# Two chained feed-forward layers after pooled attention: converted words in their own place, sums on VectorE, loads in another order

## The chip, the core and the metric

The kernel runs on one core of a Trainium2 chip. The metric is the device time of one execution in microseconds (us), as the median of three timed runs. A separate execution was taken with the hardware profiler, and all rows below are from that one.

## What is computed

Attention with keys and values that are first averaged over groups of eight positions, then two feed-forward layers, each a product, an activation and a second product:

```python
x = attention(q, mean8(k), mean8(v))          # 4608 tokens x 512
h = x @ w_in;   g = np.maximum(0.01 * h, h);  x = g @ w_out      # d_ff 2048
h = x @ w_in2;  g = np.where(h >= 1, h, np.where(h <= -1, 0.0, (h + 1) ** 2 / 4))
out = g @ w_out2
```

The weights come in as 64-bit words and are converted on the chip. Each value is split into a high part that TensorE can take and the rest, so one product is three matmuls: high by high, low by high, high by low.

## The kernel before

The program is one list of instructions written out by hand, in four phases. The first (to 574.5 us) does attention and x @ w_in block by block. The second (`Blocks.run` of layer 0) does g @ w_out, the third (`Second.first_phase`) x @ w_in2, the fourth (`Blocks.run` of layer 1) g @ w_out2. The last three use a scheme with 7 products of half blocks in place of 8; it needs sums and differences of quarter blocks beside the products.

**Second and fourth phase.** The 4608 tokens are four pairs of 512-column blocks (r = 0 to 3) and one pair of 256-column blocks, called the short pair here (r = 4). A pair has 7 positions (one product each, order `ORDER2`) of 8 units, so 56 units; a unit is 6 matmuls of 512 columns in the second phase, 12 of 256 in the fourth, and 6 of 256 in either short pair. In step u of `run` the program issues unit u's matmuls, then `hi(u + 5)` (ScalarE rounds the source, L1084), then `lo(u + 4)` (VectorE subtracts, L1089), then a sum of quarter blocks for a later unit (`g_sum`): for even f, and for all f of the first pair, VectorE adds in place 7 units ahead (L1069); for odd f of the other pairs GpSimd issues a DMA that accumulates, 10 units ahead (L1067). `g_load` (L1050) brings activations from DRAM, `fetch` (L1009) weights. After each product, `post` copies or adds its banks into output tiles (`out_tile`, places `spare[0]` to `spare[3]`) and stores them.

**Conversion beside the second phase.** `during(u)` converts w_out2 in 32 halves, one every 5 units: `bits_load` (L98) into a tile of the pool `raw`; 3 units later `convert`, whose first two steps are ScalarE's (L630, L631), then three of VectorE (L633 to L637) and one of GpSimd (L641); then `f32_store` (L146). `convert` writes into a second tile of the same pool, which has three buffers, so a later load waits until an earlier half's store has landed. In the short pair `during` also prepares the third phase: weights (`w1_fetch`, L723), `x_load`, sums (`x_sum`, GpSimd, L761) and splits (`x_split`, L718, L719).

**Third phase.** Six pairs of 768 columns with 8 cycles each, 48 cycles; a cycle has 7 slots, one product of 6 matmuls of 384 columns each. `after(cycle, slot)` holds the copies, additions (L885) and activations (L899, L904, L910) of a slot and the stores of their results (L913); `put(cycle, slot, ...)` adds work to a slot behind these. Put there are: the remaining weights `w1_fetch(12)` to `(27)`; `x_load`, `x_sum` and `x_split` for the next pair; and the sums and splits of w_out2, two of its eight parts f per pair: `w2_load` (L774), 5 slots later `w2_sums` (four on GpSimd, L783 to L786), from 7 slots on seven times `w2_split` (ScalarE L615, VectorE L618 or L620, store L797), one per slot; two tiles hold two splits each, so the fifth waits for the store of the first two. The end of the phase loads the fourth's first weights and activations.

Engines take their instructions in the program's order, SyncE (SP) its DMAs too: a DMA whose source or place is not ready holds all later ones.

Of the kernel before, what the change touches and what calls it, by code (L numbers as in the profile page):

```python
# [17 lines left out]
P = 128  # L18
# [15 lines left out]
STORES_LATE = 6  # L34

# [4 lines left out]
def attention_moe_moe2(ctx: ExitStack, tc: tile.TileContext, qT, kT, v, k01, v01, w_in1, w_out1, w_in2, w_out2, out):  # L40
# [648 lines left out]
    class Second:  # L689
# [6 lines left out]
        def __init__(self, free):  # L696
# [9 lines left out]
            self.n_t = self.n_x2 = 0  # L706
# [105 lines left out]
        def during(self, u):  # L812
            i, step = divmod(u - 7 * self.NJ + 4, 5)
            job = self.halves[i] if 0 <= i < len(self.halves) else None
            if step == 0:
                if 0 < i <= len(self.halves):
                    next(self.turn)
                if job:
                    bits_load(*job, raw_tile)
            elif step == 1 and 0 < i <= len(self.halves):  # L820
                f32_store(*self.halves[i - 1])
            elif step == 3 and job:
                self.turn = convert(*job, raw_tile)
                next(self.turn)
            elif step == 4 and job:
                next(self.turn)
# [5 lines left out]
            for at, f, *args in (  # L832
# [9 lines left out]
                if n == at:  # L842
                    f(*args)

# [70 lines left out]
        def first_phase(self):  # L915
            for t in range(EARLY, 28):
                self.put((t - EARLY) // 4 - 1, 1 + (t - EARLY) % 4, self.w1_fetch, t)
            for p in range(1, self.NPAIR):
                c = self.NJ * (p - 1)
                for cycle, slot, f, *args in (  # L920
                    (4, 2, self.x_load, p),
                    (5, 2, self.x_split, p, 0, 0), (5, 3, self.x_split, p, 0, 1),
                    (5, 4, self.x_sum, 1), (5, 6, self.x_sum, 3), (6, 1, self.x_sum, 2),
                    (6, 2, self.x_split, p, 2, 0), (6, 3, self.x_split, p, 2, 1), (6, 4, self.x_sum, 4),
                    (6, 4, self.x_split, p, 1, 0), (6, 6, self.x_split, p, 1, 1),
                    (7, 0, self.x_split, p, 3, 0), (7, 1, self.x_split, p, 3, 1),
# [499 lines left out]
```

## Time and profile before

| | |
|---|---|
| timed runs | 1677.17, 1678.49, 1684.18 us, median 1678.49 |
| profiled execution | 1684.41 us, of it span 1682.6 us |
| busy TensorE (PE), VectorE (DVE), ScalarE (ACT), GpSimd (POOL) | 1621.6, 1189.0, 975.9, 476.1 us |
| matmuls | 9324 |
| mean granted TensorE clock | 0.989 |

The busy time of PE counts a matmul from its start to its modelled end, also where it was slow; so the time that can be won is read from how many matmuls a stretch holds and the pace at which undisturbed ones follow each other. The chain of waits is the work that ended last, followed back from the end. A row of the timeline merges neighbours of one line (xN), with the time from the first's start to the last's end.

### The profile page before, as it was taken

To read this page: it belongs to the slowest core of one execution; us is meant where nothing else is said; L and a number is where in the kernel's file an instruction comes from. 1 tells how busy PE (TensorE), PEld (TensorE's weight loads), DVE (VectorE), ACT (ScalarE), POOL (GpSimd) and SP (SyncE) were. 2 spreads that over 40 slices of the span, in tenths; PEclk is the share of its full clock that TensorE was granted. 3 is DMA by queue.
4 is the path that set the end of the run, shared out by engine and by line. 5 is a ranking of instruction groups with operands and counts; after the bars stand their busy time and mean duration, and the time that the engine had idled before them with its cause. 6 is when DMAs were issued, how large, how long until landed. Compare 5 with 4: busy or idle time off the path is not lost.

```text
span 1682.6 us, 28605 instructions
## 1 busy us (share of the span) xinstructions
PE 1621.6 (96%) x9324; PEld 1449.2 (86%) x9324; DVE 1189.0 (71%) x2351; ACT 975.9 (58%) x2113; POOL 476.1 (28%) x604
## 2 busy tenths in 40 slices
PE   6899999999999999999998999999999899999998
PEld 4678787788788888888787899999999899999998
DVE  6968877877863388989786556765664786766766
ACT  4656555556554345665554577887776545454545
POOL 3524433443431004443334221221110012232323
PEclk9999999999999999999999999999999999999999
DMA  7557776778666798897869676556347977777744
GB/s 220 179 162 245 240 240 226 253 234 254 224 210 222 297 338 226 243 254 235 232 181 291 254 258 221 184 201 234 126 152 238 344 261 177 202 157 207 154 126 104
DMA packets 229973, 370.48 MB, mean 220 GB/s; under 512 B 26752, under 2 KB 108672, under 8 KB 229824
## 3 DMA queue, kind: packets, MB, share of 16 engines
q1 hardware_dynamic: 211392, 339.30, 60.2%
q0 software_dynamic: 18432, 29.37, 10.7%
q8 instruction: 73, 1.20, 0.3%
q14 instruction: 76, 0.62, 0.1%
HBM read 196.61 MB, written 142.61 MB: 202 GB/s over the span
## 4 chain that ended last, share of the span: by engine, by line
PE 71%; DVE 11%; DMA 9%; issue 3%; ACT 3%; POOL 2%; SPq 1%; DVEq 0%; ACTq 0%; POOLq 0%
PE u L1126 21%; PE u L1117 14%; PE Y L866 6%; PE h L587 6%; PE h L588 6%; PE h L589 6%; PE V L866 4%; PE X L866 4%; DMA m<-g 2%; DMA w2x<-wdo 1%; PE sc L431 1%; DMA w2d<-w2o 1%; DMA wb1o<-in_moe_w_out_dram 1%; PE tm L490 1%; DVE m L1089 1%
## 5 line engine op out<-in xcount | busy, mean ns | idle before, releaser
L1089 DVE TENSOR_TENSOR m<-m,m 128x512 fp32r<-128x512 f32 (+1 forms) x560 | 383.5, 699 | 176.4 <-ACT m L1084 163.6
L1084 ACT ACTIVATE m<-m 128x512 fp32r<-128x512 f32 (+1 forms) x560 | 324.9, 588 | 314.3 <-PE u L1126 147.5
L1126 PE MATMUL u<-v,m 128*128 128x256 f32 x3024 | 365.4, 284 | 3.5 <-ACT m L1084 3.3
L1126 PEld LDWEIGHTS u<-v,m 128*128 128x128 f32 x3024 | 364.6, 193 | 4.3 <-ACT m L1084 3.5
L1117 PE MATMUL u<-m,v 128*128 128x512 f32 (+1 forms) x1680 | 353.6, 372 | 9.8 <-ACT m L1084 5.6
L1117 PEld LDWEIGHTS u<-m,v 128*128 128x128 f32 x1680 | 296.2, 190 | 67.2 <-DVE m L1089 7.8
L587 PE MATMUL h<-xh,w0i 128*128 128x512 f32 x448 | 183.1, 409 | 0.8 <-ACT t L595 0.8
L588 PE MATMUL h<-xl,w0i 128*128 128x512 f32 x448 | 176.4, 394 | 1.8 <-DVE xl L175 1.8
L589 PE MATMUL h<-xh,w0i 128*128 128x512 f32 x448 | 176.3, 394 | 0.0
L1067 POOL DMA_DIRECT2D m<-m x128 | 112.3, 1101 | 174.0 <-DVE m L1089 148.2
L595 ACT ACTIVATE t<-h 128x512 f32<-128x512 f32 x144 | 86.0, 597 | 121.2 <-PE h L589 63.6
L1234 POOL TENSOR_TENSOR o<-o,o 128x512 f32<-128x512 f32 x36 | 62.2, 1754 | 323.9 <-DVE o L1228 323.8
L1069 DVE TENSOR_TENSOR m<-m,m 128x512 f32<-128x512 f32 (+1 forms) x192 | 127.5, 664 | 0.0
L467 POOL TENSOR_TENSOR at<-at,r 128x32 f32<-128x32 f32 (+3 forms) x160 | 72.1, 472 | 156.1 <-DVE r L464 124.4
L587 PEld LDWEIGHTS h<-xh,w0i 128*128 128x128 f32 x448 | 85.0, 190 | 20.2 <-issue 1.8
L589 PEld LDWEIGHTS h<-xh,w0i 128*128 128x128 f32 x448 | 84.7, 189 | 18.6
L588 PEld LDWEIGHTS h<-xl,w0i 128*128 128x128 f32 x448 | 84.9, 189 | 17.8 <-DVE xl L175 2.7
L866 PE MATMUL Y<-xs,v 128*128 128x384 f32 x432 | 87.2, 339 | 5.9 <-DVE p L885 4.6
L866 PE MATMUL X<-xs,v 128*128 128x384 f32 x432 | 86.7, 335 | 0.6 <-ACT Y L879 0.6
L866 PE MATMUL V<-xs,v 128*128 128x384 f32 x432 | 86.6, 334 | 0.0
L866 PEld LDWEIGHTS Y<-xs,v 128*128 128x128 f32 x432 | 75.9, 189 | 8.8 <-DVE p L885 6.2
L885 DVE TENSOR_TENSOR q<-V,q 128x384 f32<-128x384 f32 x48 | 26.6, 555 | 80.3 <-ACT q L879 80.3
(261 smaller groups left out, 2732.5 us busy)
## 6 DMA issues: line engine op xcount, KB each, us to landing
m<-g SPq DMA_DIRECT2D x256, 256.0 KB
g<-t SPq DMA_DIRECT2D x144, 256.0 KB
m<-m POOLq DMA_DIRECT2D x96, 256.0 KB, 5.5
wf<-v0o SPq DMA_DIRECT2D x56, 256.0 KB
wi<-v1i SPq DMA_DIRECT2D x56, 256.0 KB
v<-wf SPq DMA_DIRECT2D x28, 512.0 KB
v<-wi SPq DMA_DIRECT2D x28, 512.0 KB
w2d<-w2o SPq DMA_DIRECT2D x56, 256.0 KB
```

The lines of the kernel that those rows point to most:

```text
L467: nc.gpsimd.tensor_tensor(out=t, in0=t, in1=r[0:n].to_broadcast([n, 4, w]), op=ALU.mult)
L587: nc.tensor.matmul(ph, wh[:, c], xh, start=k == 0, stop=False)
L588: nc.tensor.matmul(ph, wh[:, c], xl, start=False, stop=False)
L589: nc.tensor.matmul(ph, wl[:, c], xh, start=False, stop=k == KT - 1)
L595: nc.scalar.activation(out=t, in_=h_t.pop(f), func=AF.Prelu, alpha=0.01)
L866: nc.tensor.matmul(ps, w[:, c], x[k, i], start=begin and k == n == 0, stop=k == 1 and n == 2, skip_group_check=True,)
L1067: nc.gpsimd.dma_start(out=t, in_=x, accum_op=ALU.add)
L1069: nc.vector.tensor_tensor(out=t, in0=x, in1=t, op=ALU.add)
L1084: nc.scalar.activation(out=self.s[u][0], in_=self.unit_source(u), func=AF.Copy)
L1089: nc.vector.tensor_tensor(out=lo, in0=self.unit_source(u), in1=hi, op=ALU.subtract)
L1117: nc.tensor.matmul(banks[b][:, at:at + n], w[:, c], x, start=fresh and at == 0 and i == 0, stop=end and i == 2, skip_group_check=True,)
L1126: nc.tensor.matmul(ps, a[:, c], w, start=fresh and tt % 2 == 0 and i == 0, stop=end and i == 2, skip_group_check=True,)
```

## The change

Five edits, all in phases two to four; TensorE's instructions and their order stay as they are. (1) `convert` in `during` writes into a tile of its own, `cuts` (two halves, in `spare[3]`), and the load of a half is issued 8 units ahead of `convert` rather than 3; the output tile that stood in `spare[3]` goes to `spare[0]` (`i % 3`). (2) In the short pair all sums are VectorE's, in both layers. (3) `w1_fetch(12)` to `(27)` come one every 2.5 slots instead of four a cycle; the w_out2 work moves from pairs 0 to 3 to pairs 1 to 4, with one slot more between load, sums and splits; `x_load`, sums and splits move up to 3 slots. (4) The fourth phase's first weights come one every 5 slots, its first `g_load`s one per slot, and 11 of them (`FIRST`) two per unit in the first six units. (5) In layer 1 the weights of `run` come at f = 4 to 7 rather than 0 to 3.

```diff
+FIRST = [((2, 1), f) for f in (5, 6, 7)] + [((1, 1), f) for f in range(8)]
@@ during
-            i, step = divmod(u - 7 * self.NJ + 4, 5)
...
+            for at, what in ((0, "load"), (8, "convert"), (9, "next"), (10, "next"), (11, "store")):
+                i, step = divmod(u - 7 * self.NJ + 8 - at, 5)
...
+                    bits_load(*job, raw_tile)
+                elif what == "convert":
+                    self.turn = convert(*job, self.cut_tile)
...
+        def cut_tile(self, shape, dt, name):
+            if self.cuts is None:
+                self.cuts = wpool.tile([P, 2, 512], dt, tag=self.spare[3], name="cuts")
+            self.n_cut += 1
+            return self.cuts[:, self.n_cut % 2]
@@ first_phase
-                self.put((t - EARLY) // 4 - 1, 1 + (t - EARLY) % 4, self.w1_fetch, t)
+                n = 5 * (t - EARLY) // 2
+                self.put(n // 7 - 1, n % 7, self.w1_fetch, t)
...
-                    (6, 2, self.x_split, p, 2, 0), (6, 3, self.x_split, p, 2, 1), (6, 4, self.x_sum, 4),
+                    (6, 2, self.x_split, p, 2, 0), (6, 3, self.x_split, p, 2, 1),
+                    (6, 5, self.x_split, p, 1, 0), (6, 6, self.x_split, p, 1, 1), (7, 0, self.x_sum, 4),
...
-                n = 7 * self.NJ * (f // 2) + 13 * (f % 2) + 3
-                for at, step, *args in ((0, self.w2_load), (5, self.w2_sums), *((7 + i, self.w2_split, i) for i in range(7))):
+                n = 7 * self.NJ * (f // 2 + 1) + 14 * (f % 2) + 3
+                for at, step, *args in ((0, self.w2_load), (6, self.w2_sums), *((8 + i, self.w2_split, i) for i in range(7))):
...
+            for t in range(8):
+                n = 6 + 5 * t
+                self.put(self.STEPS - self.NJ + n // 7, n % 7, self.b2.fetch, t)
             for f in range(self.NJ):
-                self.put(*((end - 3, f) if f < 4 else (end - 1, 2)), self.b2.g_load, 0, (2, 2), f)
-                self.put(end - 1, 3 if f < 4 else 6, self.b2.g_load, 0, (2, 1), f)
+                self.put(*((end - 3, f) if f < 4 else (end - 1, (2, 3, 5, 6)[f - 4])), self.b2.g_load, 0, (2, 2), f)
+            for f in range(5):
+                self.put(end, (1, 2, 4, 5, 6)[f], self.b2.g_load, 0, (2, 1), f)
...
-            by_dma = bool(f % 2 and r)
+            by_dma = bool(f % 2) and 0 < r < self.NPAIR - 1
...
+                late = 4 * self.layer
+                if r == 0 and pos < 5 and 0 <= f - late < 4:
+                    self.fetch(4 * (pos + 2) + f - late)
+                if self.layer and 2 * u < len(FIRST):
+                    for job in FIRST[2 * u:2 * u + 2]:
+                        self.g_load(0, *job)
...
-                t = self.kept[key, r] = self.out_tile(r, i)
+                t = self.kept[key, r] = self.out_tile(r, i if self.short(r) else i % 3)
```

GpSimd's list in the second phase's short pair before (m are activations, xr and x2s the third phase's x, o outputs; a DMA here is an accumulating sum):

```order
L1067 DMA m_10_6448<-m_4_6436 128x256
L1067 DMA m_11_6450<-m_5_6438 128x256
L761 TENSOR_TENSOR xr_00_9228<-xr_00_9228 128x384
L761 TENSOR_TENSOR xr_9227<-xr_9227 128x384
L761 TENSOR_TENSOR xr_00_9228<-xr_01_9230,xr_00_9228 128x384
L761 TENSOR_TENSOR xr_9227<-xr_9227 128x384
L761 TENSOR_TENSOR x2s_9384<-xr_01_9230,xr_00_9228 128x384
L761 TENSOR_TENSOR x2s_9386<-xr_9227 128x384
L1067 DMA m_8_6444<-m_34_6452 128x256
L1067 DMA m_9_6446<-m_35_6454 128x256
L1067 DMA m_10_6448<-m_36_9020 128x256
L1067 DMA m_11_6450<-m_37_9041 128x256
```

And now:

```order
L642 TENSOR_TENSOR cuts<-cuts,wb1o_1_8802 128x256
L763 TENSOR_TENSOR xr_00_9196<-xr_00_9196 128x384
L763 TENSOR_TENSOR xr_9195<-xr_9195 128x384
L763 TENSOR_TENSOR xr_00_9196<-xr_01_9198,xr_00_9196 128x384
L763 TENSOR_TENSOR xr_9195<-xr_9195 128x384
L763 TENSOR_TENSOR x2s_9353<-xr_01_9198,xr_00_9196 128x384
L763 TENSOR_TENSOR x2s_9355<-xr_9195 128x384
L1247 TENSOR_TENSOR o_0_9114<-o_0_9114,o_2_9473 128x512 x2
```

The sixteen sums of the short pair are gone from this list (six of them stand above), and VectorE's has sixteen additions more; the same holds for the fourth phase's short pair. (Lines of the changed kernel have numbers up to 13 higher.)

SyncE's list at the start of the third phase before, behind the second phase's last store (v are weights, g the results that are stored, w2x, wdo and w2d the w_out2 work):

```order
L723 DMA v_12_9662<-wi_125 128x1024
L723 DMA v_13_9673<-wi_126 128x1024
L723 DMA v_14_9675<-wi_127 128x1024
L723 DMA v_15_9683<-wi_128 128x1024
L723 DMA v_16_9712<-wi_129 128x1024
L913 DMA g_0_6100<-tX_9691 128x384
L723 DMA v_17_9725<-wi_130 128x1024
L723 DMA v_18_9737<-wi_131 128x1024
L774 DMA w2x_9739<-wdo_7097 128x512
L775 DMA w2x_9739<-wdo_8058 128x512
L723 DMA v_19_9751<-wi_132 128x1024
L913 DMA g_8_6108<-tV_9733 128x384
```

And now:

```order
L725 DMA v_12_9622<-wi_125 128x1024
L725 DMA v_13_9642<-wi_126 128x1024
L725 DMA v_14_9658<-wi_127 128x1024
L725 DMA v_15_9669<-wi_128 128x1024
L921 DMA g_0_6100<-tX_9656 128x384
L725 DMA v_16_9702<-wi_129 128x1024
L725 DMA v_17_9721<-wi_130 128x1024
L921 DMA g_8_6108<-tV_9698 128x384
L921 DMA g_8_6108<-tW_9710 128x384
L725 DMA v_18_9754<-wi_131 128x1024
L921 DMA g_1_6101<-tX_9719 128x384
L921 DMA g_0_6100<-tY_9749 128x384
```

Between two weights there are now mostly results to store, and w2x comes eight cycles later.

SyncE's list at the end of the third phase before, behind the last tX but one (m are the fourth phase's activations, g with t results that are stored):

```order
L1050 DMA m_4_13646<-g_12_6112 128x512
L1050 DMA m_5_13648<-g_13_6113 128x512
L1050 DMA m_6_13650<-g_14_6114 128x512
L1050 DMA m_7_13652<-g_15_6115 128x512
L913 DMA g_5_6105<-tY_13629 128x384
L1050 DMA m_8_13666<-g_0_6100 128x512
L1050 DMA m_9_13668<-g_1_6101 128x512
L1050 DMA m_10_13670<-g_2_6102 128x512
L1050 DMA m_11_13672<-g_3_6103 128x512
L1050 DMA m_21_13697<-g_4_6104 128x512
L1050 DMA m_21_13697<-g_5_6105 128x512
L1050 DMA m_21_13697<-g_6_6106 128x512
```

And now:

```order
L1059 DMA m_7_13656<-g_15_6115 128x512
L921 DMA g_14_6114<-tV_13623 128x384
L921 DMA g_14_6114<-tW_13637 128x384
L1059 DMA m_8_13674<-g_0_6100 128x512
L921 DMA g_7_6107<-tX_13646 128x384
L1059 DMA m_9_13679<-g_1_6101 128x512
L921 DMA g_6_6106<-tY_13669 128x384
L1059 DMA m_10_13698<-g_2_6102 128x512
L1059 DMA m_11_13703<-g_3_6103 128x512
L1059 DMA m_21_13715<-g_4_6104 128x512
L921 DMA g_15_6115<-tV_13687 128x384
L921 DMA g_15_6115<-tW_13695 128x384
```

Before, twelve loads stand together with one store among them; now the stores of tV, tW, tX and tY stand between them.

VectorE's list in the second phase, now, from the second half converted to the third, with what each waits for (DMAHW and DMASW are landings of DMAs issued by SyncE and GpSimd):

```order
L638 SCALAR_TENSOR_TENSOR cuts_7069<-wb1o0_1_7038,cuts_7069 128x256 [waits DMAHW4_49,DVE_49]
L1098 TENSOR_TENSOR m0_24_6404<-m0_9_6446,m0_21_6392 128x512 [waits DMASW1_49,Activation_49]
L1078 TENSOR_TENSOR m0_34_6452<-m0_18_6282,m0_34_6452 128x512 [waits DMAHW5_49]
L1098 TENSOR_TENSOR m0_24_6404<-m0_10_6448,m0_24_6404 128x512 [waits Activation_49]
L1098 TENSOR_TENSOR m0_29_6457<-m0_11_6450,m0_28_6456 128x512 [waits DMASW2_49,Activation_49]
L1078 TENSOR_TENSOR m0_12_6226<-m0_18_6282,m0_12_6226 128x512 [waits DMAHW7_49]
L1098 TENSOR_TENSOR m0_31_6461<-m0_34_6452,m0_30_6460 128x512 [waits Activation_49]
L1098 TENSOR_TENSOR m0_33_6472<-m0_35_6454,m0_32_6471 128x512 [waits DMASW3_49,Activation_49]
L1078 TENSOR_TENSOR m0_12_6226<-m0_1_6320,m0_12_6226 128x512
L634 TENSOR_SCALAR cuts_7069<-cuts_7069 128x256 [waits Activation_49]
L635 TENSOR_SCALAR cuts_7069<-cuts_7069 128x256 [waits DVE_49]
L638 SCALAR_TENSOR_TENSOR cuts_7069<-wb1o1_0_7096,cuts_7069 128x256 [waits DMAHW0_49,DMAHW7_49,DVE_49,Pool_49]
```

The last step of the second half into cuts waits for one landing, that of its load; the third half's, which takes the first's place again, for two.

## Rows read from the trace of the kernel before

**Rows 1.** Busy time by stretch; the header line names the columns.

```profile
core 0: us, PE busy (x) PEld busy (x) DVE busy (x) ACT busy (x) POOL busy (x), PEclk, DMA share, GB/s
574.50:883.90 309.40, 307.44 (x1345) 253.28 (x1345) 267.90 (x436) 175.03 (x323) 99.91 (x98) 0.99 0.84 248
883.90:937.70 53.80, 45.93 (x337) 42.76 (x337) 39.17 (x85) 26.22 (x69) 24.32 (x22) 0.97 0.83 240
937.70:1009.50 71.80, 65.97 (x362) 64.75 (x362) 35.06 (x70) 48.83 (x114) 13.25 (x14) 0.95 0.79 288
1009.50:1071.10 61.60, 59.38 (x338) 58.06 (x338) 40.90 (x78) 49.40 (x118) 13.73 (x14) 1.00 0.59 205
1071.10:1131.30 60.20, 59.06 (x337) 58.02 (x336) 39.82 (x78) 49.36 (x118) 14.17 (x14) 1.00 0.61 210
1131.30:1193.90 62.60, 59.84 (x338) 57.94 (x337) 39.67 (x78) 49.21 (x118) 13.41 (x14) 1.00 0.58 202
1193.90:1252.30 58.40, 58.40 (x338) 58.26 (x337) 33.47 (x64) 45.10 (x104) 7.14 (x6) 1.00 0.40 136
1252.30:1309.20 56.90, 54.93 (x313) 53.83 (x313) 26.68 (x54) 39.88 (x91) 0.00 (x0) 1.00 0.67 224
1309.20:1320.00 10.80, 7.30 (x48) 6.53 (x47) 4.31 (x8) 5.49 (x11) 0.00 (x0) 0.91 0.81 260
...
1637.70:1678.30 40.60, 40.55 (x338) 40.34 (x337) 30.12 (x71) 22.77 (x56) 15.68 (x17) 1.00 0.53 108
```

**Rows 2.** Longest pieces of the chain of waits: start, us, what, matmuls in it.

```profile
574.71 204.01 PE u L1117 x900
...
1215.03 2.08 PE Y L866 x12
...
1318.24 360.02 PE u L1126 x2986
```

**Rows 3.** The chain of waits in the second phase, 798 to 815 us.

```profile
798.58 7.10 DMA wdo<-wc1o
805.74 8.33 DMA wb1o<-in_moe_w_out_dram
814.15 0.44 ACT wc1o L630
```

**Rows 4.** ScalarE's longest wait in 883.9 to 937.7: us, times, longest.

```profile
ACT m L1084 <- DMA m<-m: 11.6, 5, 5.0
```

**Rows 5.** VectorE's timeline in the short pair: start, us, what, idle before.

```profile
910.13 6.51 DVE L1089 TENSOR_TENSOR m<-m,m 128x256 fp32r<-128x256 f32 x7
...
929.75 1.09 DVE L1089 TENSOR_TENSOR m<-m,m 128x256 fp32r<-128x256 f32 x3
```

**Rows 6.** GpSimd's timeline in the short pair.

```profile
911.38 1.19 POOL L761 TENSOR_TENSOR xr<-xr,xr 128x384 f32<-128x384 f32 x1
...
915.98 3.57 POOL L1067 DMA_DIRECT2D m<-m  x4
```

**Rows 7.** The chain of waits at the third phase's start: start, us, what.

```profile
958.34 5.34 DMA w2d<-w2o
```

**Rows 8.** TensorE's longest wait in 937.6 to 1309.1: us, times, longest.

```profile
PE Y L866 <- DVE p L885: 7.9, 10, 1.7
```

**Rows 9.** The chain of waits in the third phase's second pair.

```profile
1026.32 4.00 DMA w2d<-w2o
...
1031.73 3.14 DMA w2x<-wdo
...
1037.79 0.70 POOL w2s L786
```

**Rows 10.** The chain of waits where the fourth phase begins.

```profile
1303.60 5.64 DMA m<-g
...
1309.30 6.51 DMA g<-tV
```

More of the change, by code (lines that the diff above doesn't have):

```diff
@@ L705, in __init__ @@
             self.w2d = [dram.tile([P, self.NJ, 2, 256], F32, name=f"w2d{pos}") for pos in range(7)]
-            self.n_t = self.n_x2 = 0
+            self.n_t = self.n_x2 = self.n_cut = 0
+            self.cuts = None
             self.plan = {}
@@ L812, in during @@
         def during(self, u):
-            i, step = divmod(u - 7 * self.NJ + 4, 5)
-            job = self.halves[i] if 0 <= i < len(self.halves) else None
-            if step == 0:
-                if 0 < i <= len(self.halves):
-                    next(self.turn)
[L818 to L826, printed above, removed]
+            for at, what in ((0, "load"), (8, "convert"), (9, "next"), (10, "next"), (11, "store")):
+                i, step = divmod(u - 7 * self.NJ + 8 - at, 5)
+                if step or not 0 <= i < len(self.halves):
+                    continue
+                job = self.halves[i]
+                if what == "load":
+                    bits_load(*job, raw_tile)
+                elif what == "convert":
+                    self.turn = convert(*job, self.cut_tile)
+                    next(self.turn)
+                elif what == "next":
+                    next(self.turn)
+                else:
+                    f32_store(*job)
             n = u - 56 * (NT // 1024)
@@ L920, in first_phase @@
                 for cycle, slot, f, *args in (
[L921 to L926 removed]
+                    (4, 4, self.x_load, p),
+                    (5, 4, self.x_split, p, 0, 0), (5, 5, self.x_split, p, 0, 1),
+                    (5, 6, self.x_sum, 1), (6, 1, self.x_sum, 3), (6, 3, self.x_sum, 2),
+                    (6, 2, self.x_split, p, 2, 0), (6, 3, self.x_split, p, 2, 1),
+                    (6, 5, self.x_split, p, 1, 0), (6, 6, self.x_split, p, 1, 1), (7, 0, self.x_sum, 4),
+                    (7, 1, self.x_split, p, 3, 0), (7, 2, self.x_split, p, 3, 1),
                     (7, 3, self.x_split, p, 4, 0), (7, 4, self.x_split, p, 4, 1),
@@ L949, in first_phase @@
                         f(*args)
-                if cycle >= self.STEPS - self.NJ:
-                    for t in range(28):
-                        if t < 8 and (2 * t + 1) // 7 == cycle % self.NJ:
-                            self.b2.fetch(t)
             for slot in range(6):
@@ L1134, in run @@
                     self.g_load(0, (2, 1), f)
-            for f in range(self.NJ):
-                self.g_load(0, (1, 1), f)
+                for f in range(self.NJ):
+                    self.g_load(0, (1, 1), f)
             self.hi(3)
@@ L1149, in run @@
                     self.g_sum(u + ahead, ahead)
-                if r == 0 and pos < 5 and f < 4:
-                    self.fetch(4 * (pos + 2) + f)
+                late = 4 * self.layer
[4 more added lines that the diff above has]
+                        self.g_load(0, *job)
                 if prod == 7:
```

## The prediction

> **What bounds the kernel now.** I read first the busy time by stretch [rows 1] and the pieces of the chain of waits [rows 2]. TensorE is busy nearly all the time and its list does not change, so all that can be won is time in which its matmuls follow each other more slowly than they can. Undisturbed, they come every 204.01 / 900 = 0.2267 us in the second phase, 2.08 / 12 = 0.1733 in the third and 360.02 / 2986 = 0.1206 in the fourth [rows 2]; for the second phase's short pair, whose matmuls have the 256 columns of the fourth's, I take 0.1206 too. The length of a stretch [rows 1] less its matmuls at that pace is what was lost in it:
>
> - second phase, long pairs: 309.4 - 1344 x 0.2267 = 4.7 us
> - its short pair: 53.8 - 336 x 0.1206 = 13.3
> - third phase, first pair with the four products ahead of it: 71.8 - 360 x 0.1733 = 9.4
> - pairs two to five (336 matmuls, 58.2 us each): 3.4, 2.0, 4.4 and 0.2
> - last pair: 56.9 - 312 x 0.1733 = 2.8
> - start of the fourth phase: 10.8 - 48 x 0.1206 = 5.0
> - its short pair: 40.6 - 336 x 0.1206 = 0.1
>
> In sum 45.3 us, 2.7% of the execution. In the stretches that lost most the granted clock is 0.97, 0.95 and 0.91 on average [rows 1], since after an idle piece it stood at the lower level (1.2 of 2.4 GHz) for a while; that cost lies in the losses and goes with them. The first phase isn't touched.
>
> **The change part by part.**
>
> *Converted words.* A half's store took 7.10 us, the next load behind it 8.33, and only then could ScalarE start on the half, at 814.15 [rows 3]; behind that one instruction stood the rounding of the next units, and the 4.7 us were lost there. With a place of its own the load waits for no store, and it is issued 8 units of 6 x 0.2267 = 1.36 us ahead, 10.9 us, against 4.1 before. 8.33 us fit in. No instruction is added. SyncE's list still has the store wait for GpSimd, 3 units behind `convert`, and holds later loads for that as before. Cost of moving the output tile into `spare[0]`: its next user starts 8 units after the pair's end and the store is put in at the 4th, 5 x 1.36 = 6.8 us for a store of 256 KB; the two DMAs of [rows 3] took 7.10 and 8.33, so ScalarE may wait 0.3 to 1.5 us there, which its lead of some four units (5.4 us) hides; uncovered it would be four times 1.5. I take 0.5 us left of 4.7: gain **4.2** (bounds 0 to 4.7).
>
> *Short pairs.* The waits of ScalarE for accumulating DMAs, 11.6 us [rows 4], go: the four of the list that stand behind six GpSimd additions are issued only at 915.98 [rows 6]. In their place VectorE gets 16 additions. Three instructions of 256 columns took 1.09 us, 0.36 each [rows 5], so 5.8 us on 39.2 busy [rows 1]: 45.0, against 40.5 of TensorE. So VectorE is late next. It works up to four units ahead (4 x 0.72 = 2.9 us) and the last four units have no subtraction left, which puts the loss between 45.0 - 40.5 - 2.9 = 1.6 and 4.5 us; I take 3.5, near the upper end, since splits for the third phase crowd units 32 to 43. Gain **9.8** (bounds 0 to 11.7). What hides nothing there: while GpSimd added 128x384 tiles of x (1.19 us each [rows 6]), seven VectorE instructions took 6.51 us, 0.93 each in place of 0.36 [rows 5]; those slow ones are in the 39.2 already. In the fourth phase's short pair VectorE has 30.1 + 5.8 = 35.9 us of work beside 40.6 [rows 1]: no cost (bounds 0 to 3).
>
> A rule of the Trainium skill speaks against this part: "SBUF — State Buffer", section "Who interferes with whom", says that a VectorE instruction with two inputs in SBUF and a GpSimd instruction that reads SBUF exclude each other, the later one waiting for the whole of the other. The 0.93 us agree with it. By the rule, all additions that meet GpSimd's would be held, and the short pair would come to the second rival below.
>
> *Third phase, first pair.* A store of w_out2's splits took 5.34 us [rows 7], and ScalarE's fifth split stood behind it, with the next activations behind that. This work now starts a pair later, so in the first pair there is nothing to stand behind. What is left on the queues are 16 weights of 512 KB, one every 2.5 x 6 x 0.1733 = 2.6 us (202 GB/s), and four results of 192 KB a cycle of 7.28 us (108 GB/s): 310 GB/s against the 288 that the stretch moved on average at a DMA share of 0.79 [rows 1]. That is close to full, so stores of results will take some us, but their tiles come round only after about 11 us. I take 0.4 us left: gain **9.0** (bounds 5 to 9.4).
>
> *Pairs two to five.* The w_out2 work is now in all four; the fifth, without it, lost 0.2 [rows 1], so moved unchanged it would cost 3.3 a pair, the mean of 3.4, 2.0 and 4.4. It isn't unchanged. TensorE's wait is for VectorE's addition p, 7.9 us in 10 times [rows 8], and p stood behind a split in VectorE's list: the fifth to seventh split wait for stores (4.00 us), the first of the second part for GpSimd's fourth sum, which ends at 1038.49 because its load came at 1031.73 and took 3.14 [rows 9]. One slot later (1.04 us) these splits stand behind p and not ahead of it: the fifth to seventh from slots 14 to 16 to slots 15 to 17, where p's slot is 17; the first of the second part from slot 23 to 25, where p's slot is 24. The waits stay, but behind them are instructions that nobody needs for two slots. The x work moves up to three slots; its two-input VectorE work still meets GpSimd's additions, so some of it stays. I take 1.0 us a pair: 4.0 left of 10.0, gain **6.0** (bounds -3.2, all four at 3.3, to 9).
>
> *Last pair and fourth phase.* Twelve loads of 256 KB in a row and a store of tV behind them: 5.64 and 6.51 us [rows 10], while ScalarE stood waiting for that tile. Now nine loads lie between the stores over the last two cycles, and eleven come in the first six units of 12 x 0.1206 = 1.45 us. 2 x 256 KB a unit are 362 GB/s, more than the 260 seen there [rows 1], so they will run late; but a sum needs its load 5 to 8 units after the issue. Gain **2.3** of 2.8 and **4.0** of 5.0 (bounds 0 to 7.8 for both).
>
> **Sum.** 4.2 + 9.8 + 9.0 + 6.0 + 2.3 + 4.0 = 35.3 us, 10.0 of 45.3 being left. The profiled execution took 1684.41 us with its span of 1682.6, so it would take 1649.1. It stands 5.9 us over the median of the runs, 1678.49; I put the gain on the median: **1643.2 us**. Should the 5.9 us lie in the waits that go, the gain is 29.4 and the median 1649.1.
>
> **The rivals.**
>
> *VectorE takes the wait over.* If every addition in the short pairs goes at 0.93 us and not 0.36 [rows 5], 16 of them are 14.9 us, VectorE has 54.1 beside 40.5, and the short pair loses 13.6 as before; in the fourth phase 30.1 + 14.9 = 45.0 against 40.6 adds up to 4. Then 35.3 - 9.8 - 4 = 21.5 and 1657. For it: the slow seven. Against: GpSimd's additions fill 1.2 us each, six of them, and its DMAs are gone.
>
> *The w_out2 waits come along.* Pairs two to five lose 3.3 each or somewhat more: 6.0 + 3.2 less, 1652.4. For it: the waits for store and load are as long as before. Against: the order by slot.
>
> *The loads are not the cause.* If the queues are full whatever the order, the first pair, the last pair and the fourth phase keep half of their 17.2 us: 1651. If none of the five edits did what it says, the time would stay at 1678.
>
> *Slower: the tile `cuts` makes VectorE wait.* If a half's last VectorE step into `cuts` waits for the landing of the half before it, whose store is put in 3 units (4.1 us) earlier, a store of 7.10 us [rows 3] costs 3.0 us, 32 times 96; VectorE has 41.5 us free in the long pairs [rows 1], so 54 go to the end, and the time would be 1678.5 - 31.1 + 54 = 1701. It decides from a mean landing of 4.1 + (41.5 + 31.1) / 32 = 6.4 us on. Against: in the changed list the second half waits for one landing, its load's, and the third for two, its load's and that of the first half's store, 8 units (10.9 us) old.
>
> **How the numbers follow.** Forecast 0.62, 1636 to 1650. VectorE takes over 0.14 (1657); w_out2 waits come along 0.11 (1652); loads not the cause 0.08 (1651), no effect 0.02; slower 0.03 (1701). The range holds 0.62, the two cases at 1651 and 1652 and most of that at 1657: below, all but 2.8 of the 45.3 us gone gives 1636, above 1658. A measurement of this kernel can tell about 0.5%, 8.4 us, from no change: below 1670.1 lies all but the last two cases, 0.95; same 0.02; slower 0.03.
>
> **What would show it.** TensorE's list is the same, so the stretches can be laid side by side: second phase's long pairs near 305 us, short pair 44, third phase 72 - 9 = 63 for its first stretch and 59 each for the next four. ScalarE's wait for wb1o and for m<-m should be gone, VectorE nearly full in the short pair, the granted clock 1.00 in all stretches but the short pair. It is wrong where a pair of the third phase still loses 2 us or more to p, where the short pair takes 48 or more, or where the fourth phase's first 48 matmuls take over 8.

## The result and the profile after

The changed kernel takes 1661.67 us (median of six runs, 1657.52 to 1663.90), the kernel before 1680.93 beside it; ratio 0.9886, 95% interval 0.9863 to 0.9908. So it is faster, but by 19.3 us (1.1%) and not by 35.3; 1661.67 lies 3.7 us above the range. The profiled execution took 1663.90 us, 20.5 less than that of before.

Busy time by stretch, with the same borders as [rows 1], a moved start apart:

```profile
core 0: us, PE busy (x) PEld busy (x) DVE busy (x) ACT busy (x) POOL busy (x), PEclk, DMA share, GB/s
576.90:881.60 304.70, 304.70 (x1346) 252.30 (x1345) 269.23 (x436) 177.49 (x323) 100.80 (x96) 1.00 0.85 250
881.60:930.10 48.50, 44.71 (x338) 42.27 (x337) 42.06 (x101) 27.45 (x69) 13.30 (x8) 0.97 0.66 231
930.10:994.00 63.90, 62.98 (x362) 62.66 (x361) 30.60 (x56) 44.24 (x99) 7.42 (x6) 0.99 0.73 247
994.00:1054.40 60.40, 58.84 (x337) 58.15 (x337) 40.53 (x78) 49.33 (x117) 14.13 (x14) 1.00 0.60 209
1054.40:1113.20 58.80, 58.74 (x338) 58.17 (x337) 41.14 (x78) 49.47 (x117) 14.03 (x14) 1.00 0.63 215
1113.20:1174.50 61.30, 59.37 (x339) 58.14 (x338) 40.74 (x78) 49.34 (x117) 14.06 (x14) 1.00 0.59 206
1174.50:1234.80 60.30, 59.15 (x338) 58.20 (x338) 40.35 (x78) 49.18 (x117) 14.35 (x14) 1.00 0.61 210
1234.80:1291.00 56.20, 54.88 (x313) 53.93 (x312) 26.59 (x54) 40.41 (x91) 0.00 (x0) 1.00 0.70 222
...
1617.40:1657.80 40.40, 40.40 (x338) 40.24 (x336) 34.35 (x87) 22.63 (x55) 2.80 (x2) 1.00 0.19 60
```

Length of a stretch before less its length now, beside the forecast:

| stretch | before | after | gain | forecast |
|---|---|---|---|---|
| second phase, long pairs | 309.4 | 304.7 | 4.7 | 4.2 |
| its short pair | 53.8 | 48.5 | 5.3 | 9.8 |
| third phase, first pair | 71.8 | 63.9 | 7.9 | 9.0 |
| pairs two to five | 242.8 | 240.8 | 2.0 | 6.0 |
| last pair | 56.9 | 56.2 | 0.7 | 2.3 |
| fourth phase ahead of its short pair | 328.5 | 326.4 | 2.1 | 4.0 |

The sum is 22.7 of 35.3; two thirds of what is missing lie in the short pair and in pairs two to five. (The second phase also began 2.4 us later, at 576.9 and not 574.5, behind a first phase that is the same: hence 20.5.) Two of the prediction's signs of being wrong came: the short pair took 48.5 us, and the fourth pair of the third phase lost 3.0 us, about 2 of them to p. The last one did not: the fourth phase's first 48 matmuls took about 6 us, but its loss lay just behind them. Three new places show in the trace of after.

In the **short pair** VectorE's subtractions are slow beside GpSimd's additions of x, and later VectorE stands for GpSimd. Two timelines (start, us, what, idle before), VectorE's and GpSimd's:

```profile
902.41 6.53 DVE L1098 TENSOR_TENSOR m<-m,m 128x256 fp32r<-128x256 f32 x7
...
925.64 0.69 DVE L1232 SCALAR_TENSOR_TENSOR o<-u,o 128x512 f32<-128x512 f32 x1 [2.42 <-POOL o L1247]
```

```profile
903.67 1.19 POOL L763 TENSOR_TENSOR xr<-xr,xr 128x384 f32<-128x384 f32 x1
...
919.08 6.53 POOL L1247 TENSOR_TENSOR o<-o,o 128x512 f32<-128x512 f32 x2 [10.75 <-DVE o L1241]
```

The first seven are 0.93 us each, as in [rows 5]. The second wait is one that the prediction has nowhere: two additions into output tiles (L1247) end the short pair's products on GpSimd, 3.3 us each, and VectorE's next step (L1232) reads what they read and writes it.

In the **third phase** 6.7 us are lost in the seventh cycle of the five pairs that prepare the next one's x (1.2, 1.8, 0.2, 2.1 and 1.4; here and below read from the starts of the matmuls less 0.1733 us each; the expectations below put this sum at 6.4). The chain of waits of the second pair, and the waits of the whole phase (us, times, longest):

```profile
1033.39 6.17 DMA g<-tV
...
1039.64 0.49 ACT tX L907
...
1044.11 1.35 DVE xs L721
1045.46 0.48 DVE p L893
...
1045.99 0.44 PE Y L874
```

```profile
ACT tX L907 <- DMA g<-tV: 8.4, 4, 2.6
...
PE Y L874 <- DVE p L893: 6.1, 6, 1.6
...
ACT w2o L616 <- DMA w2d<-w2o: 2.4, 5, 0.7
```

ScalarE's wait for w_out2's stores was 11.3 us in the third phase before and is 2.4; its wait for a store of tV, where it puts the next tX into the same tile, has grown from 5.3 to 8.4. In the **fourth phase** VectorE waits for a store of the third:

```profile
1294.89 3.46 DMA g<-tY
...
1298.47 0.70 DVE m L1098
```

### The profile page after: what moved, and what is told of

The parts are those of the page before. It is cut to its first block, busy times and chain, and to the rows that moved or that the text cites. A ratio compares the mean times of both kernels' runs of the same rounds, so it can differ in the third digit from the quotient of the medians.

```text
span 1661.9 us, 28512 instructions
## 1 busy us (share of the span) xinstructions
PE 1613.5 (97%) x9324; PEld 1446.6 (87%) x9324; DVE 1199.9 (72%) x2383; ACT 979.3 (59%) x2113; POOL 454.5 (27%) x572
## 4 chain that ended last, share of the span: by engine, by line
PE 80%; DVE 10%; ACT 3%; DMA 3%; issue 3%; POOL 1%; SPq 0%; DVEq 0%; ACTq 0%; POOLq 0%
PE u L1135 22%; PE u L1126 20%; PE Y L874 7%; PE h L588 6%; PE h L589 6%; PE h L590 6%; PE X L874 5%; PE V L874 4%; PE sc L432 1%; PE tm L491 1%; DVE vs L338 1%; DVE vr L359 1%; DMA g<-tV 1%; DMA wb0i<-in_moe_w_in_dram 1%; PE av L508 1%
## 5 line engine op out<-in xcount | busy, mean ns | idle before, releaser
L1126 PE MATMUL u<-m,v 128*128 128x512 f32 (+1 forms) x1680 | 349.5, 370 | 3.8 <-DVE m L1098 3.6
L1247 POOL TENSOR_TENSOR o<-o,o 128x512 f32<-128x512 f32 x36 | 63.8, 1799 | 354.2 <-DVE o L1241 352.8
L1078 DVE TENSOR_TENSOR m<-m,m 128x512 f32<-128x512 f32 (+1 forms) x224 | 141.0, 629 | 0.0
L1076 POOL DMA_DIRECT2D m<-m x96 | 84.0, 1036 | 136.4 <-DVE m L1098 108.5
L874 PEld LDWEIGHTS X<-xs,v 128*128 128x128 f32 x432 | 76.3, 189 | 0.0
```

Source lines behind the costliest of these rows:

```text
L874: nc.tensor.matmul(ps, w[:, c], x[k, i], start=begin and k == n == 0, stop=k == 1 and n == 2, skip_group_check=True,)
L1076: nc.gpsimd.dma_start(out=t, in_=x, accum_op=ALU.add)
L1078: nc.vector.tensor_tensor(out=t, in0=x, in1=t, op=ALU.add)
L1126: nc.tensor.matmul(banks[b][:, at:at + n], w[:, c], x, start=fresh and at == 0 and i == 0, stop=end and i == 2, skip_group_check=True,)
```

## Experiments

All are the changed kernel with one edit, but for the one with all corrections. Each single edit was run once, so stretches of its profile are compared. How far a stretch moves that an edit leaves alone is the measure for a difference: the third phase took 360.8 to 362.4 us in the five such profiles, the short pair 47.3 to 48.5 in nine, the fourth phase ahead of its short pair 324.9 to 327.4 in eleven.

### Third phase: is it GpSimd?

My first theory came from the slow subtractions: GpSimd's additions hold VectorE's, and p comes late. Three runs tested it.

```diff
-                engine = nc.vector if what == 4 else nc.gpsimd
+                engine = nc.vector if what == 4 or p else nc.gpsimd
```

> The changed kernel, but in the third phase the six subtractions of x per pair that GpSimd did are VectorE's. In the changed kernel the third phase takes 930.1 to 1291.0 = 360.9 us against 2016 x 0.1733 = 349.4 at pace; 6.4 of the 11.5 lost lie in the seventh cycle of the five pairs that split x for the next one. Theory (GpSimd's additions of 1.0 to 1.3 us hold VectorE's two-input ones, so that p comes late): these 6.4 us fall to 1 or less, third phase 355 to 356, although VectorE has 30 instructions more. Rival (splits of x stand ahead of p whoever adds): 6.4 stay or grow by the six additions a pair, third phase 361 to 364. Rival (w_out2's waits came along): the loss would have to lie in the second to fifth cycle, and stays.

```diff
-                    (5, 6, self.x_sum, 1), (6, 1, self.x_sum, 3), (6, 3, self.x_sum, 2),
+                    (5, 5, self.x_sum, 1), (5, 6, self.x_sum, 3), (6, 1, self.x_sum, 2),
...
-                    (6, 5, self.x_split, p, 1, 0), (6, 6, self.x_split, p, 1, 1), (7, 0, self.x_sum, 4),
-                    (7, 1, self.x_split, p, 3, 0), (7, 2, self.x_split, p, 3, 1),
+                    (6, 4, self.x_sum, 4), (6, 4, self.x_split, p, 1, 0), (6, 6, self.x_split, p, 1, 1),
+                    (7, 0, self.x_split, p, 3, 0), (7, 1, self.x_split, p, 3, 1),
```

> The changed kernel, but in the third phase x's subtractions on GpSimd come at slots (5,5), (5,6) and (6,1) and VectorE's at (6,4), and the splits that follow up to one slot earlier, as in the kernel before (the load and the first split stay where the change put them). Theory (GpSimd holds VectorE wherever the two meet): the 6.4 us of the seventh cycles stay in sum between 2 and 8, in other pairs or slots, since the kernel before lost 0.8 and 1.3 us there in two of its pairs. Rival (the change's new slots alone are bad): the seventh cycles lose under 1 us in all five pairs, third phase about 355.

```diff
-                engine.tensor_tensor(out=to, in0=a, in1=b, op=ALU.subtract)
+                if p:
+                    for _ in range(3):
+                        nc.gpsimd.memset(to, 0.5)
```

> The changed kernel, but in the third phase each of GpSimd's subtractions of x is replaced by three writes of a constant into the same tile, which read nothing; VectorE's list stays as it is (the next pairs' x is not computed). Theory, in the form that it is GpSimd's reading beside VectorE's two-input instructions that holds these: VectorE's splits and copies stay at 0.55 us each and the seventh cycles lose 1 us or less, third phase 355 to 356, as in the kernel with all on VectorE. Rival (what counts is that GpSimd is late with the data, or busy): if the three writes take as long as one subtraction, 6.4 us stay. If they take much less, a loss that goes tells only the theory and the lateness together, and the durations of VectorE's instructions beside them decide.

| kernel | third phase | lost in the seventh cycles | ScalarE for tV | TensorE for p |
|---|---|---|---|---|
| changed | 360.9 us | 6.7 | 8.4 | 6.1 |
| VectorE adds | 359.9 | 6.4 | 8.7 | 5.6 |
| old slots | 362.7 | 6.8 | 8.5 | 6.0 |
| GpSimd only writes | 356.5 | 2.0 | 9.0 | 1.0 |

The theory fell with the first run. VectorE's timeline there, in the second pair's seventh cycle, has no slow instruction left, and p is late all the same:

```profile
1038.82 0.56 DVE L721 TENSOR_TENSOR xs<-xr,xs 128x384 fp32r<-128x384 f32 x1 [3.11 <-ACT xs L720]
1039.30 1.02 DVE L763 TENSOR_TENSOR xr<-xr 128x384 f32<-128x384 f32 x2
...
1041.63 1.02 DVE L763 TENSOR_TENSOR xr<-xr,xr 128x384 f32<-128x384 f32 x2
...
1043.51 0.55 DVE L893 TENSOR_TENSOR p<-Y,p 128x384 f32<-128x384 f32 x1
```

Ahead of it VectorE stood idle for 3.11 us behind a split of ScalarE's, which stood behind tX. The second run says that the slots of the sums and splits make no difference to the seventh cycles. In the third GpSimd was busy as long (nine writes in 4.0 us), VectorE's splits beside them took 0.56 us and not 1.35, and most of the loss went though tX waited longer than ever:

```profile
ACT tX L911 <- DMA g<-tV: 9.0, 4, 3.8
...
PE Y L878 <- ACT q L891: 1.7, 2, 1.1
```

Three of these four waits, 1.1 to 2.3 us, then cost 0.3 us or less each. The longest, 3.8 us in the second pair, still cost 1.8, of which TensorE waited 1.1 for ScalarE's q directly. So a store that is late enough costs by itself; with waits as in the changed kernel (1.7 to 2.6 us) it takes two things together in most pairs: ScalarE late behind a store, and VectorE with more or slower work between the late split and p.

### Third phase: the loads of x

Ahead of the late store of tV on SyncE's list stand the four loads of the next x, 384 KB each. One run spreads them, one takes them off that queue.

```diff
-                    (4, 4, self.x_load, p),
+                    (4, 4, self.x_load, p, [(0, 0)]), (4, 6, self.x_load, p, [(1, 0)]),
+                    (5, 1, self.x_load, p, [(0, 1)]), (5, 3, self.x_load, p, [(1, 1)]),
```

> The changed kernel, but the four loads of x for the next pair (384 KB each, issued within 1.5 us at slot (4,4)) come at slots (4,4), (4,6), (5,1), (5,3). New theory, since the 6.4 us stayed when VectorE did the subtractions and nearly went when nothing was read: it takes two things together, ScalarE's tX that stands up to 2.6 us for the landing of an older store of tV (8.4 us in 4 waits), which landed late because the four loads were queued ahead of it, and VectorE's extra or slowed work between the late split and p. Without the bunch of loads that wait falls to under 2 us in all, the seventh cycles lose 2 us or less of 6.4, third phase 355 to 357 against 360.9. Rival (VectorE's list ahead of p is too long by itself, GpSimd's slowing or the six subtractions being enough): 6.4 stay, whatever the stores do. Rival (queues full): tX's wait only moves to other cycles and the third phase stays at 360 to 361.

```diff
-                    nc.sync.dma_start(out=t[:, 0:2 * NH], in_=x2[2 * r + k][:, c])
+                    engine = nc.gpsimd if p else nc.sync
+                    engine.dma_start(out=t[:, 0:2 * NH], in_=x2[2 * r + k][:, c])
```

> The changed kernel, but the four loads of x for the next pair are issued by GpSimd, at the same slot, so they are not ahead of the stores on SyncE's queue, while as many bytes move at the same time. Theory (order in SyncE's queue makes tV's store late): tX's wait for tV falls from 8.4 us to under 3 and the seventh cycles lose 2 us or less of 6.4. Rival (the bytes themselves make the store late, whichever queue they are on): the store of tV beside the loads still takes 5 us or more, tX's wait stays above 5 and 6.4 us stay. GpSimd's issues take some 0.9 us each; it has nothing else to do at that slot.

Spread, the third phase took 355.0 us and its seventh cycles lost 1.1; on GpSimd's queue 355.2 and 0.95. The waits of the first, in which GpSimd adds and slows VectorE as before:

```profile
ACT tX L906 <- DMA g<-tV: 1.1, 2, 0.8
...
PE Y L873 <- DVE p L892: 1.0, 2, 0.7
```

The second run isn't as clean as it was meant to be: GpSimd has nothing else to do, so it issued the loads as soon as their tiles were free, not at their slot (for the first pair at 932 us, four cycles early). In the second pair they came at the same place, and what changed there is that the store no longer stands behind them. SyncE's issues in the changed kernel, then in this one:

```profile
1030.94 2.35 SPq L740 DMA_DIRECT2D xr<-x  x4
1033.39 0.38 SPq L921 DMA_DIRECT2D g<-tV  x1
```

```profile
1028.25 0.40 SPq L800 DMA_DIRECT2D w2d<-w2o  x1
1028.74 0.41 SPq L922 DMA_DIRECT2D g<-tV  x1
```

It began that pair 2.2 us earlier, so the store of tV is issued 2.4 us sooner within the pair. The two runs agree that the loss goes when this store is on time.

The order on the queue isn't what made these stores late. In the second run the next store, of tW, is issued on SyncE's queue at 1031.39 us with no load ahead of it there, 0.46 us behind GpSimd's last load. By the updates of its semaphore in the trace it landed 6.47 us later; in the changed kernel, behind the loads on the one queue, 6.19. The other three pairs show the same: 5.5, 5.1 and 6.1 us against 5.2, 5.1 and 5.6. The store of tV landed after 2.4 us (2.5, 4.7 and 2.4 in the other pairs) because it was issued beside the first load and not behind the fourth. So the rival of that run, the bytes under way, accounts for how long a store takes, and the loss went because tV's store got ahead of them. "DMA: Bandwidth & Descriptors" of the Trainium skill, section "Issuing engines are not separate DMA queues", says that a transfer issued by another engine saves the time of issuing only. This trace agrees: the saving is the 2.35 us in which SyncE issued the loads. For the phase that was worth 5.7 us.

### The short pair

```diff
+                engine = nc.vector if self.short(r) else nc.gpsimd
...
-                    nc.gpsimd.tensor_tensor(out=t[:, k], in0=t[:, k], in1=q[:, k], op=ALU.add)
+                    engine.tensor_tensor(out=t[:, k], in0=t[:, k], in1=q[:, k], op=ALU.add)
```

> The changed kernel, but the two additions of GpSimd into the output tiles at the end of the second phase's short pair (128x512, 919.1 to 925.6 us) are VectorE's. The short pair took 48.5 us, 8.0 over 336 x 0.1206. Theory (add_minus waits 2.4 us for GpSimd's slow additions, VectorE stops, TensorE waits 2.0 us and then runs at the lower clock for 3.4 us): 2.5 to 4 of the 8.0 us go, short pair 44.5 to 46, and the half-speed piece at 927 with them. What stays is the stretch with x's subtractions. Rival (VectorE is full and only its amount of work counts): two additions more make it 1.4 us longer, 49 to 50.

The same, and the six subtractions of x too:

```diff
-                engine = nc.vector if what == 4 else nc.gpsimd
+                engine = nc.gpsimd if p and what != 4 else nc.vector
```

> The changed kernel, but in the second phase's short pair all of GpSimd's additions are VectorE's: six subtractions of x (128x384) and two additions into output tiles (128x512); GpSimd then does nothing there. With the two alone the short pair lost 6.1 us of the 8.0. Theory (GpSimd's additions hold VectorE's, seven in 6.5 us in place of 2.5): another 1.5 to 3.5 us go, short pair 43.5 to 45.5, since VectorE's six instructions of 0.47 to 0.55 us cost 3 us and the seven slow ones gave 4 us. Rival (VectorE is full, the amount of its work decides): its busy time of 42 us grows by 3 beyond what the slow ones give back, and the short pair takes 46.9 (as with the two alone) to 49.

Undone, the sums by DMA:

```diff
-            by_dma = bool(f % 2) and 0 < r < self.NPAIR - 1
+            by_dma = bool(f % 2) and 0 < r < self.NPAIR - self.layer
```

> The changed kernel, but in the second phase's short pair the sums of odd f are accumulating DMAs of GpSimd again (in the fourth phase VectorE's, as in the changed kernel). Theory (those behind GpSimd's subtractions of x are issued late and hold ScalarE): the short pair goes back to 52 to 54 us from 48.5, and ScalarE again waits over 8 us for m<-m. Rival (the short pair lost its time to VectorE being held by GpSimd, which both kernels have): 48 to 50, and 48.5 - 53.8 came from the conversions' end or the loads.

The short pair's stretch in the three, in this order (columns as above):

```profile
880.40:926.90 46.50, 43.49 (x338) 41.03 (x337) 43.09 (x103) 27.53 (x69) 6.77 (x6) 1.00 0.69 241
```

```profile
880.10:925.30 45.20, 42.88 (x338) 40.92 (x337) 41.81 (x109) 27.49 (x69) 0.00 (x0) 1.00 0.71 248
```

```profile
881.30:937.20 55.90, 47.65 (x337) 44.62 (x336) 37.15 (x85) 25.90 (x69) 25.67 (x23) 0.93 0.82 238
```

With DMA sums it is 55.9 us, above the 52 to 54 expected, and ScalarE waits 16.1 us for m<-m (11.6 before): the edit did what it says, and is worth 7.4. GpSimd's two output additions on VectorE bring 2.0, less than expected, the granted clock 1.00 from 0.97. Not all of the 2.0 is theirs. In four runs that leave these additions with GpSimd (constants, spread loads, other tiles, w_out2 back) TensorE has the same wait of 1.9 us and yet a granted clock of 1.00 over the pair, which takes 47.3; with the loads spread:

```profile
879.40:926.70 47.30, 43.53 (x337) 41.04 (x337) 41.90 (x101) 27.45 (x69) 13.29 (x8) 1.00 0.69 237
```

So 0.8 us are the additions' own, and 1.2 the clock that fell behind the wait in the changed kernel and did not in these runs. With the six subtractions too another 1.3 go, and VectorE's busy time falls from 43.1 to 41.8 with six instructions more, since none is slowed any longer. That agrees with "SBUF — State Buffer" of the Trainium skill, section "Who interferes with whom": two SBUF inputs on VectorE and a reading GpSimd exclude each other, and one that only writes does no harm (0.56 us beside the constants above).

### The fourth phase's start

```diff
-                (12, 13, 14, 27, 32, 33, 34, 35, 30, 31, 28, 29),
+                (12, 13, 14, 27, 32, 33, 34, 35, 36, 37, 28, 30),
```

> The changed kernel, but the parts of units 4 and 5 of the fourth phase lie in tiles whose last results were stored three or more cycles earlier, not in those of the last tY and tW. Theory (VectorE's lo(4) waits 3.0 us for the store of the last tY, TensorE then 1.9 us and runs at the lower clock for 3.4 us after): the 2.4 us that the fourth phase's long pairs lost behind their first 48 matmuls fall to 0.5 or less. Rival (the activations' loads are late anyway, 4.7 to 8.7 us from issue to landing there): another wait, for m<-g, takes their place and 1.5 us or more stay.

The first 11.2 us of the fourth phase, in the changed kernel and in this one:

```profile
1291.00:1302.20 11.20, 9.46 (x65) 9.05 (x65) 7.40 (x14) 6.39 (x13) 0.00 (x0) 0.87 0.99 349
```

```profile
1289.80:1301.00 11.20, 11.17 (x93) 10.96 (x92) 10.40 (x19) 7.69 (x15) 0.00 (x0) 1.00 0.99 339
```

28 matmuls more in the same time are 28 x 0.1206 = 3.4 us. The loads weren't late; the tile was.

### What moving w_out2 was worth

```diff
-                n = 7 * self.NJ * (f // 2 + 1) + 14 * (f % 2) + 3
+                n = 7 * self.NJ * (f // 2) + 14 * (f % 2) + 3
```

> The changed kernel, but the w_out2 work is back in the third phase's pairs 0 to 3, in the changed kernel's slots. The first pair lost 9.4 us before and 1.2 after the change, which moved w_out2 out of it and spread the weights. Theory of the prediction (w_out2's stores, queued among the weights, hold ScalarE's split and what stands behind it): 3 to 8 us of the 8.1 come back in the first pair, at its third and fourth cycles; the fifth pair keeps only the seventh cycle's loss. Rival (the weights' spread was the cure, four a cycle having crowded the queue): the first pair stays within 1.5 us of what it is, 63.9 us.

```diff
-                n = 7 * self.NJ * (f // 2 + 1) + 14 * (f % 2) + 3
-                for at, step, *args in ((0, self.w2_load), (6, self.w2_sums), *((8 + i, self.w2_split, i) for i in range(7))):
+                n = 7 * self.NJ * (f // 2 + 1) + 13 * (f % 2) + 3
+                for at, step, *args in ((0, self.w2_load), (5, self.w2_sums), *((7 + i, self.w2_split, i) for i in range(7))):
```

> The changed kernel, but w_out2's steps have the old distances (sums 5 slots behind the load, splits from 7 on, the second part 13 slots behind the first); they stay in pairs 1 to 4. Theory of the prediction (the splits that wait for stores and for GpSimd's sums stood ahead of p): the third and fourth cycles of these pairs lose 1.5 to 2.5 us a pair again (1.5 and 0.8, 0.7 and 1.1, 1.6 and 1.3 in the kernel before), 6 to 10 us in the four, on top of the seventh cycles. Rival (these losses went because the weights are no longer on the queue, or because the x steps moved): under 2 us come back in the four pairs.

Back in the first pair, w_out2 costs that pair 8.6 us (72.5 against 63.9) although the weights are spread. It was expected to cost 3 to 8, in the third and fourth cycles; 2.2 are lost in the third and 5.5 in the fifth. The chain of waits, where it lost most:

```profile
956.96 5.63 DMA v<-wi
...
962.72 4.63 DMA w2d<-w2o
...
967.78 0.47 ACT p L887
```

This run also shows the loads of x without w_out2 beside them. In its fifth pair tV's store is issued 37.2 us into the pair (39.8 in the changed kernel), no tX waits for it, and the seventh cycle loses 0.2 us and not 1.4. So there the four loads alone were not enough. Whether it is w_out2's stores ahead of them on SyncE's list that hold the issue back wasn't tried.

In the old slots pairs two to five take 250.1 us against 240.8, with 11.9 lost in their third and fourth cycles against none (6 to 10 were expected). TensorE's waits for p over the third phase are 10.9 us in 13 times:

```profile
ACT w2o L616 <- POOL w2s L788: 12.6, 8, 3.1
...
PE Y L874 <- DVE p L893: 10.9, 13, 2.4
```

### All corrections together

The loads spread, the short pair on VectorE, the places of the fourth phase, and in the short pair x's splits moved out of the units in which VectorE also has a sum:

```diff
-                (32, self.x_split, 0, 1, 0), (33, self.x_split, 0, 1, 1),
-                (34, self.x_split, 0, 2, 0), (35, self.x_split, 0, 2, 1), (36, self.x_sum, 4),
...
+                (32, self.x_split, 0, 1, 0), (41, self.x_split, 0, 1, 1),
+                (42, self.x_split, 0, 2, 0), (43, self.x_split, 0, 2, 1), (44, self.x_sum, 4),
...
+            for n in range(4):
+                self.put(-1, (1, 2, 4, 5)[n], self.x_split, 0, 5 + n // 2, n % 2)
```

> The changed kernel with the three corrections together: loads of x two slots apart in the third phase, the short pair's additions all on VectorE, parts of the fourth phase's units 4 and 5 in tiles whose results were stored earlier; besides, x's splits for the first pair of the third phase avoid units 33 to 40 of the short pair (there VectorE has a subtraction, a sum and a split per unit, 0.34 + 0.34 + 0.47 = 1.15 us against TensorE's 0.72), four of them coming behind TensorE's first products of the third phase. By the single runs the losses were 20.2 to 22.1 us in all; 5.5 go in the seventh cycles, 3.2 in the short pair, 3 in the fourth phase: 1661.7 - 11.7 = 1650. If the crowd in units 33 to 40 is what is left of the short pair (0.3 a unit from 909 to 914 us and 0.8 at its end), another 1.5 to 3 us go: 1647 to 1649. If the corrections get in each other's way, 1652 to 1656.

Five runs gave 1646.59 to 1654.35 us, median 1652.13; ratio to the kernel before 0.9804, interval 0.9784 to 0.9824, below that of the change. The short pair and the third phase:

```profile
886.30:929.40 43.10, 41.71 (x337) 40.62 (x336) 40.61 (x105) 25.51 (x65) 0.00 (x0) 1.00 0.73 260
929.40:1285.20 355.80, 353.56 (x2019) 348.97 (x2018) 224.70 (x426) 284.70 (x657) 63.56 (x62) 1.00 0.65 222
```

The short pair gained 2.1 us more than with all on VectorE alone, so the crowded units were that much of it. The median lies above the 1647 to 1650 expected, but the corrections did not get in each other's way: against the changed kernel's profile the short pair is 5.4 us shorter, the third phase 5.1, and the fourth phase ahead of its short pair 3.5 (322.9), 14.0 in all; the first phase of this profile is 4.7 us longer.

## Why the prediction was wrong

**Conversions** (4.2, got 4.7): right; the long pairs run without a gap, PE busy 304.70 of 304.70, and ScalarE's waits for wb1o, 21.2 us before, are gone. Whether the place or the earlier load did it wasn't tried apart.

**Short pair** (9.8, got 5.3): the step on ScalarE's waits was right (the DMA run). The failing step is "VectorE is late next ... 3.5". It weighed sums of busy time over the whole pair and let VectorE's lead cover the rest. VectorE's busy time came out at 42.1 us, below the 45.0 of that sum, and yet the pair lost 8.0. VectorE was full in one piece of it (0.93 us a subtraction beside GpSimd, then 1.15 us of work a unit against TensorE's 0.72):

```profile
902.00:909.00 7.00, 6.28 (x45) 5.37 (x44) 7.00 (x10) 4.12 (x10) 5.75 (x5) 1.00 1.00 349
909.00:915.00 6.00, 5.03 (x37) 4.35 (x36) 6.00 (x16) 2.50 (x6) 0.00 (x0) 1.00 0.65 266
```

And the 2.42 us for GpSimd's output additions weren't in the sum. By the runs, of 8.0 us lost the output additions were 0.8, the lower clock behind them 1.2, the subtractions of x 1.3, the crowded units 2.1. The first rival, all additions at 0.93 us (the prediction's paragraph on the Trainium skill's rule calls it the second), did not come: the short pair lost 8.0 and not 13.6, and the fourth phase's took 40.4.

**First pair** (9.0, got 7.9): right in its cause (w_out2 put back: 8.6 us); the 1.2 left are its seventh cycle.

**Pairs two to five** (6.0, got 2.0): the reading of w_out2's slots was right, and worth more than I gave it: 9.3 us against the old slots, nothing of the splits' wait left in the third and fourth cycles. The failing step is what I let stay: "its two-input VectorE work still meets GpSimd's additions, so some of it stays. I take 1.0 us a pair". That meeting alone costs 0.2 a pair (loads spread). What cost most of the 6.7 in five pairs was a store that I had not looked at: tV's, issued behind the four loads of x. With that store on time 5.6 of the 6.7 went. I had followed w_out2's DMAs through SyncE's queue, and of the x steps only the work on the engines. The change puts these loads two slots, 2.1 us, nearer to the tX that needs the tile; that this is what made the loss grow wasn't tried by itself. Such a wait was to be seen before; the chain of waits of that kernel, in the fourth pair's seventh cycle, reads

```profile
1173.20 6.19 DMA g<-tY
...
1179.46 0.54 ACT tW L899
```

That cycle lost 1.3 us. The second pair's lost 0.8, with a wait of 1.2 us for a store of tV, but there the chain does not pass through the store.

**Last pair** (2.3, got 0.7): 1.8 us stand in its last cycle in every kernel run here, TensorE's waits for q of ScalarE and for p of VectorE. The products of the next cycle that fill those slots elsewhere don't exist there. That is argued, not tried; I had put the loss to the loads without reading its rows.

**Fourth phase** (4.0, got 2.1): the 6.51 us for a store of tV [rows 10] were to go with the loads ahead of it. That store no longer holds anyone, and the next one whose tile the fourth phase takes, tY's, took its place with 3.46 us; the run with other tiles shows it, and gains 3.4. (The 2.1 are not sharp: in the eleven profiles that leave it alone this stretch varies by 2.5 us.) What I had not asked is which store lands last once the queue is clear.

**Sum and base.** The gain fell short by 16.0 us, and the sizes above make 12.6 of them. 2.4 lie in the first phase, ahead of the change's first instruction, and 1.2 between the gain of the profiled executions (20.5) and that of the medians (19.3). The forecast's base, 1678.49 where six runs give 1680.93, puts another 2.4 us between 1643.2 and 1661.67. One sum was off without weight: of the 17.2 us of the case at 1651 the forecast had left 1.9, so half kept would have given 1649.9.

## What to carry to other kernels

A load that is moved changes which small stores are issued behind its bytes, on its own queue or another's: list the stores issued within the next few microseconds, and for each the instruction that takes its tile next; that engine is where the time shows. Judge an engine's lead piece by piece, by its work per step against the bottleneck's, and not by its busy share over a stretch. A wait found by name (GpSimd slows VectorE) is a cause only if taking it away brings the time back; here it didn't. With the store on time the slowing cost 1.1 us of 6.7, and with the slowing gone the late store still cost 2.0; the rest took both.

## What the runs showed of the hardware

A store of 192 KB that is issued behind four loads of 384 KB lands 5 to 7.6 us after its issue, against 1.9 us without them, and 5.1 to 6.5 us where the loads went out on another engine's queue (stores of tV in the changed kernel, of tW with the loads on GpSimd's queue, by their semaphores in the traces).

The first phase, identical in all kernels here, ends at very different times. The longest pieces of the chain that open the second phase, in the changed kernel, with w_out2 put back, and with all corrections:

```profile
577.07 322.65 PE u L1126 x1494
```

```profile
572.01 322.65 PE u L1126 x1494
```

```profile
581.79 322.65 PE u L1126 x1494
```

That is a spread of 9.8 us, 0.6% of the execution, beside a piece that takes 322.65 us each time; it is why stretches were compared here and not single times. It may also be why the profiled run of the last kernel is the slowest of its five; the other four have no trace. What in the first phase varies was not looked into.
